# Turning the last x tile of each later chunk on the DMA queue instead of on TensorE, with its values moved one step

## The chip, the cores and the metric

The kernel runs on one core of a Trainium2 chip. The metric is the device time of one execution in microseconds (us). All runs told here are fast runs (granted TensorE clock 0.998 to 1.0). A ratio is the mean time of one kernel's fast runs over that of the other's fast runs of the same rounds, so it isn't quite the ratio of the medians that stand beside it; the 95% interval follows in brackets.

## The reference, cut to what matters

Attention over a band of 64 positions plus 8 global ones, then a gated feed-forward block with a residual:

```python
attn = softmax(where(band | is_global, scale * q @ k.T, -1e9)) @ v
x = attn.transpose(0, 2, 1, 3).reshape(4608, 512)     # B*S tokens, H*D
ffn = (gelu(x @ w_gate) * (x @ w_val)) @ w_out
out = x + sigmoid(x @ w_res) * ffn
```

(Shortened. B, H, S, D = 8, 8, 576, 64; the feed-forward width is 1536.)

## The kernel before: the parts that matter

The 4608 tokens are worked through in nine chunks (c = 0 to 8) of four tiles of 128 tokens. While TensorE does the feed-forward block of chunk c, the attention of chunk c+1 is slipped in between. For each tile t of the next chunk, `values` multiplies the attention weights with v into the PSUM tile `nd`, VectorE divides `nd` and writes `xtok` (tokens on partitions), and `turn_x` makes the transposed `xt`, which the next chunk's `g_ps` and `v_ps` products read.

```python
psn = ctx.enter_context(tc.tile_pool(name="psn", bufs=1, space=PSUM))   # nd: one buffer of two banks
...
def local_values(c, t):
    if split(c, t):          # tiles 0 and 2 of chunk 0: two banks of the matmul ring
        nds = [psm.tile([128, 512], F32, name=f"nd{hf}", tag="mm") for hf in range(2)]
    else:
        nd = psn.tile([128, 2, 512], F32, name="nd", tag="nd")
...
def turn_x(c, t):
    mine = xt[c % 2][:, :, 128 * t:128 * t + 128]
    if c > 1 and t < 3:
        nc.sync.dma_start(mine, xtok[c % 2][:, t, :], transpose=True)
        return
    tx = pss.tile([128, NKT, 128], BF16, name="tx", tag="sc")
    for kk in range(NKT):
        nc.tensor.transpose(tx[:, kk, :], xtok[c % 2][:, t, 128 * kk:128 * kk + 128], ident)
    (nc.vector.tensor_copy if c or t == 3 else nc.scalar.copy)(mine, tx)
...
# the tail of chunk c: 16 steps work_f[n] of four matmuls each,
# gate, third, third, third for each of the four tiles
for n in range(16):
    for w in jobs[n]:
        w()
    work_f[n]()
```

In the traces here TensorE and SyncE start their instructions in the order in which they were emitted (in the first experiment below, a turn whose data are ready stands 2.4 us behind a store). To turn a tile is to transpose it. A gate's four matmuls write the PSUM tile `r_ps`, and a tile's three thirds add up in `f_ps`. The last third of tile t (work_f[4t + 3]) also emits VectorE's `prb`, GpSimd's `ob` and the output store on SyncE's queue, which is the queue of the transposing DMAs too.

The softmax here doesn't subtract the row's maximum and nothing guards it: scores larger than these inputs give would overflow.

## Time and profile before

| | before |
|---|---|
| median, first three runs | 394.37 us (393.6 to 395.18) |
| span of the profiled run | 392.0 us |
| TensorE (PE) busy | 378.8 us, 97% |
| transposes of x on TensorE | 60, of which 28 for tile 3 of chunks 2 to 8 |
| from the first g_ps of chunk 2 to that of chunk 3 | 40.69 us |

The table is read from the top down: TensorE is the bound, so a change pays only by what it does to TensorE's sequence of starts. The last row is the measure that I use throughout: it holds one whole chunk with one tail, and it repeats to some hundredths of a microsecond, while whole runs differ by 1.5 us. The lines themselves stand in the prediction. In them PEld is TensorE loading weights, SPq is SyncE issuing DMAs, and instructions in a row of one kind are merged, with their count (x8). A DMA raises its semaphore sixteen times; its landing is the time of the sixteenth increment.

### The profile page before, as it was taken

What the parts mean: (1) busy time and instruction counts of PE and PEld (TensorE: products, weight loads), DVE (VectorE), ACT (ScalarE), POOL (GpSimd) and SP (SyncE); (2) the same over time, 40 slices, a digit from 0 to 9 for tenths busy, and PEclk for the clock granted to TensorE, in tenths of its full rate; (3) what the DMA queues carried; (4) which work ended last, traced back from release to release, by engine and by line L of the source; (5) the groups of instructions that cost most, each with busy time, mean ns of one, the idle gap of its engine ahead of it and who ended that gap; (6) DMA issues with size and microseconds to landing.
All of it is one profiled execution on the core that took longest, in us unless ns stands there. A gap on an engine that the chain in (4) does not pass through costs nothing.

```text
span 392.0 us, 8491 instructions
## 1 busy us (share of the span) xinstructions
PE 378.8 (97%) x3360; PEld 196.5 (50%) x3360; DVE 203.4 (52%) x446; ACT 171.1 (44%) x285; POOL 169.2 (43%) x203
## 2 busy tenths in 40 slices
PE   3989989999999999999999999999999999999996
PEld 2674555444644454445544554455445544554444
DVE  7767773547543664357444644555445534553422
ACT  6753685236333633354335533462337233633321
POOL 7878764958265424561466137712501210121012
PEclk9999999999999999999999999999999999999999
DMA  8999999699759913997399829992990310041002
GB/s 245 256 378 358 239 321 207 149 196 152 110 97 151 184 42 110 122 204 82 88 149 185 88 82 131 189 113 80 114 150 16 81 55 0 2 93 57 0 28 81
DMA packets 153002, 52.78 MB, mean 135 GB/s; under 512 B 136386, under 2 KB 143426, under 8 KB 152962
## 3 DMA queue, kind: packets, MB, share of 16 engines
q1 hardware_dynamic: 77024, 41.88, 44.4%
q0 software_dynamic: 75392, 9.84, 43.0%
q8 instruction: 26, 0.43, 0.5%
q10 hardware_dynamic: 546, 0.52, 0.4%
q14 instruction: 14, 0.11, 0.1%
HBM read 39.19 MB, written 9.44 MB: 124 GB/s over the span
## 4 chain that ended last, share of the span: by engine, by line
PE 93%; DVE 3%; ACT 2%; issue 1%; POOL 0%; DVEq 0%; POOLq 0%; ACTq 0%
PE g_ps L630 24%; PE v_ps L630 23%; PE f_ps L686 23%; PE r_ps L656 8%; PE nd L575 4%; PE sc L534 3%; PE nd L587 2%; PE ss L481 1%; PE sg L472 1%; PE tx L610 1%; PE tk L451 1%; PE sc L523 1%; PE tq L451 1%; ACT pt L541 1%; PE sn L510 1%
## 5 line engine op out<-in xcount | busy, mean ns | idle before, releaser
L639 DVE SCALAR_TENSOR_TENSOR ht<-gsb,v_ps 128x512 bf16<-128x512 bf16 x108 | 74.2, 688 | 95.3 <-PE v_ps L630 89.2
L636 ACT ACTIVATE gsb<-g_ps 128x512 bf16<-128x512 f32 x108 | 64.4, 597 | 123.1 <-PE g_ps L630 119.7
L692 POOL TENSOR_TENSOR ob<-prb,xtok 128x512 f32<-128x512 f32 x35 | 40.3, 1155 | 172.0 <-DVE prb L690 172.0
L630 PE MATMUL g_ps<-xt,wg_t 128*128 128x512 bf16 (+1 forms) x456 | 111.9, 368 | 0.0
L630 PE MATMUL v_ps<-xt,wv_t 128*128 128x512 bf16 (+1 forms) x456 | 111.9, 368 | 0.0
L686 PE MATMUL f_ps<-wo_t,ht 128*128 128x512 bf16 x420 | 100.1, 379 | 0.0
L630 PEld LDWEIGHTS <-wv_t 128*128 128x128 bf16 x456 | 43.4, 98 | 49.1
L630 PEld LDWEIGHTS <-wg_t 128*128 128x128 bf16 x456 | 43.3, 98 | 48.9 <-issue 0.3
L686 PEld LDWEIGHTS <-ht 128*128 128x128 bf16 x420 | 38.9, 98 | 38.9
L664 ACT ACTIVATE rsb<-r_ps 128x512 bf16<-128x512 f32 x36 | 21.5, 600 | 71.8 <-PE r_ps L656 71.8
L690 DVE SCALAR_TENSOR_TENSOR prb<-rsb,f_ps 128x512 f32<-128x512 bf16 x35 | 24.0, 686 | 27.5 <-PE f_ps L686 26.0
L656 PE MATMUL r_ps<-wr_t,xt 128*128 128x512 bf16 x144 | 36.8, 379 | 1.0 <-ACT rsb L664 1.0
L541 ACT ACTIVATE pt<-sc 128x512 bf16<-128x512 f32 x64 | 33.3, 615 | 4.9 <-PE sc L534 4.8
L91 POOL DMA_DIRECT2D q_st<-in_q_dram x25 | 21.5, 866 | 18.5 <-DMA qt<-q_st 18.4
L557 DVE TENSOR_TENSOR pt<-pt,maskw 128x512 bf16<-128x512 bf16 x56 | 23.2, 424 | 7.7 <-ACT pt L541 5.8
L575 PEld LDWEIGHTS <-pt 128*128 128x128 bf16 x576 | 22.0, 97 | 9.5 <-PE r_ps L656 0.7
L99 POOL DMA_DIRECT2D ve<-in_v_dram x30 | 25.5, 866 | 0.0
L600 DVE TENSOR_TENSOR xtok<-nd,rden 128x512 bf16<-128x512 f32 x34 | 23.5, 691 | 1.3
L91 POOL DMA_DIRECT2D k_st<-in_k_dram x25 | 21.1, 864 | 4.8 <-DMA kt<-k_st 4.1
L575 PE MATMUL nd<-ve,pt 128*128 128x65 bf16 x320 | 22.5, 193 | 0.6 <-DVE xtok L600 0.6
L599 DVE RECIPROCAL rden<-nd 128x8 f32<-128x8 f32 x34 | 7.0, 207 | 29.3 <-PE nd L587 29.2
L656 PEld LDWEIGHTS <-xt 128*128 128x128 bf16 x144 | 13.5, 97 | 16.0 <-issue 0.9
(174 smaller groups left out, 307.9 us busy)
## 6 DMA issues: line engine op xcount, KB each, us to landing
out_dram<-ob SPq DMA_DIRECT2D x35, 256.0 KB
vo<-ve SPq DMA_DIRECT2D x12, 260.0 KB
q_st<-in_q_dram POOLq DMA_DIRECT2D x20, 128.0 KB, 5.8
k_st<-in_k_dram POOLq DMA_DIRECT2D x20, 128.0 KB, 6.5
ve<-in_v_dram POOLq DMA_DIRECT2D x18, 128.0 KB, 7.0
wo_t<-in_k_dram SPq DMA_DIRECT2D x8, 256.0 KB
vraw<-in_q_dram SPq DMA_DIRECT2D x8, 256.0 KB
extra<-in_moe_w_out_dram SPq DMA_DIRECT2D x4, 512.0 KB
```

The lines of the kernel that those rows point to most:

```text
L91: nc.gpsimd.dma_start(dst[0:n, r, :].rearrange("p (h d) -> p h d", d=D), src[b].rearrange("h s d -> s h d")[128 * r:128 * r + n])
L99: nc.gpsimd.dma_start(t[p0:p1, c, :, 0:D], v[b].rearrange("h s d -> s h d")[s0 + p0:s0 + p1])
L541: nc.scalar.activation(sc if stay else mine, sc, ACTF.Exp, bias=0.0, scale=SCALE)
L575: nc.tensor.matmul(nds[h // 4][:, VG * (h % 4):VG * (h % 4) + VG], view(pt, 0, 128, c0, [[1, 128]]), vw, start=(h % 4 == 0 and e == 0), st ...
L600: nc.vector.tensor_tensor(xtok[c % 2][:, t, :].rearrange("p (a h d) -> p a h d", a=2, d=D), num[:, :, :, 0:D], view(rden, 0, 128, 0, [[4, ...
L630: nc.tensor.matmul(held[what][:, c0:c1], w[:, kk, 128 * j:128 * j + 128], x[:, kk, c0:c1], start=(kk == 0), stop=(kk == NKT - 1))
L636: nc.scalar.activation(held["s"], held["g"], ACTF.Gelu, bias=0.0, scale=1.0)
L639: nc.vector.scalar_tensor_tensor(ht[:, j, :], held["s"], 0.5, held["v"], ALU.mult, ALU.mult)
L656: nc.tensor.matmul(r_ps, xt[c % 2][:, kk, 128 * t:128 * t + 128], wr_t[:, kk, :], start=(kk == 0), stop=(kk == NKT - 1))
L686: nc.tensor.matmul(held["f"], ht[:, j, 128 * t:128 * t + 128], wo_t[:, j, :], start=(j == 0), stop=(j == NFF - 1))
L690: nc.vector.scalar_tensor_tensor(prb, held["r"], 1.0, held["f"], ALU.add, ALU.mult)
L692: nc.gpsimd.tensor_tensor(ob, prb, xtok[c % 2][:, t, :], ALU.add)
```

## The change

Its intent is to take the last transposes of the steady chunks off TensorE, and to let the transposing DMA start early enough that it lands before the next chunk reads it. For that, the values of tile 3 come one step earlier and each turn is emitted right behind its values.

```diff
     def turn_x(c, t):
         mine = xt[c % 2][:, :, 128 * t:128 * t + 128]
-        if c > 1 and t < 3:
+        if c > 1:
             nc.sync.dma_start(mine, xtok[c % 2][:, t, :], transpose=True)
             return
@@
             for t in range(4):
-                jobs[5 + 2 * t].append(lambda t=t: values(c + 1, t))
-                jobs[7 + 2 * t].insert(0, lambda t=t: turn_x(c + 1, t))
+                n = (5, 7, 9, 10)[t]
+                jobs[n].append(lambda t=t: values(c + 1, t))
+                jobs[n].append(lambda t=t: turn_x(c + 1, t))
```

## The prediction

> **What bounds the kernel now.** I read the page's engine rows first, then the chain that ended last, then the costliest groups for the lines that the diff touches, and last the timeline of one chunk's tail, which is where all of the change lies.
>
> ```profile
> PE 378.8 (97%) x3360; PEld 196.5 (50%) x3360; DVE 203.4 (52%) x446; ACT 171.1 (44%) x285; POOL 169.2 (43%) x203
> PEclk9999999999999999999999999999999999999999
> PE 93%; DVE 3%; ACT 2%; issue 1%; POOL 0%; DVEq 0%; POOLq 0%; ACTq 0%
> ...
> L610 PE MATMUL tx<-ident,xtok 128*128 128x128 bf16 x60 | 5.9, 219 | 0.0
> ...
> L611 DVE COPY xt<-tx 128x512 bf16<-128x512 bf16 x12 | 5.1, 424 | 7.1 <-PE tx L610 7.1
> ```
>
> TensorE is busy for 97% of the span at the full clock, and 93% of the chain that ended last is TensorE. So an instruction taken off TensorE is worth its slot there, a new hole on TensorE costs its whole length, and half-idle VectorE gives nothing back by itself. The 60 transposes have 219 ns records, but records of pipelined matmuls overlap: what counts is the distance between starts. Here is the tail in which chunk 4 makes x tiles 2 and 3 of chunk 5 (start, length, engine, operation).
>
> ```profile
> 185.49 0.39 PE L587 MATMUL nd<-vgs,gt 128*128 128x260 bf16 x2
> 185.71 1.89 PE L686 MATMUL f_ps<-wo_t,ht 128*128 128x512 bf16 x8
> 185.91 0.21 DVE L599 RECIPROCAL rden<-nd 128x8 f32<-128x8 f32 x1 [0.24 <-PE nd L587]
> 186.16 0.69 DVE L600 TENSOR_TENSOR xtok<-nd,rden 128x512 bf16<-128x512 f32 x1
> 186.94 0.34 SPq L694 DMA_DIRECT2D out_dram<-ob  x1
> 187.38 2.52 SPq L606 DMA_TRANSPOSE xt<-xtok  x2
> 187.92 0.39 PE L587 MATMUL nd<-vgs,gt 128*128 128x260 bf16 x2
> 189.87 0.39 PE L610 MATMUL tx<-ident,xtok 128*128 128x128 bf16 x4
> 190.09 2.75 PE L686 MATMUL f_ps<-wo_t,ht 128*128 128x512 bf16 x12
> 190.29 0.43 DVE L611 COPY xt<-tx 128x512 bf16<-128x512 bf16 x1 [0.30 <-PE tx L610]
> 192.69 1.03 PE L630 MATMUL g_ps<-xt,wg_t 128*128 128x512 bf16 x4
> ```
>
> The reader is to see three things. The four transposes hold TensorE from 189.87 to 190.09. The two tiles of values follow each other with eight f_ps matmuls between them (185.71 to 187.44, where the next tile's first matmul starts). And VectorE empties the first tile's nd only at 186.16 + 0.69 = 186.85; nd has one buffer, so the next tile may not start before that. With eight matmuls between, it never waits.
>
> There is one place in the kernel before where only four matmuls stand between two such tiles, in the first chunk, and it shows what the new order will look like:
>
> ```profile
> 55.91 1.02 PE L656 MATMUL r_ps<-wr_t,xt 128*128 128x512 bf16 x4
> 56.11 0.21 DVE L599 RECIPROCAL rden<-nd 128x8 f32<-128x8 f32 x1 [1.01 <-PE nd L587]
> 56.41 0.69 DVE L600 TENSOR_TENSOR xtok<-nd,rden 128x512 bf16<-128x512 f32 x1
> ...
> 57.17 0.55 PEld L575 LDWEIGHTS <-pt 128*128 128x128 bf16 x16 [0.73 <-PE r_ps L656]
> 57.20 0.19 PE L575 MATMUL nd<-vo,pt 128*128 128x65 bf16 x1 [0.27 <-PE r_ps L656]
> ```
>
> Four such matmuls take 0.86 us (spacing 0.216 us, as 189.01 to 189.87 in the tail above), so TensorE was free for the next tile at 55.91 + 0.86 = 56.77. It started at 57.20, 0.10 us after xtok ended (56.41 + 0.69 = 57.10). The row names r_ps as releaser, but VectorE's read of nd ended last. The hole is 0.43 us.
>
> **What the Trainium skill says.** "TensorE: Matmul & The Clock Gate", Part 4: PE-mode transpose, puts a 128x128 transpose at about 275 ns in a kernel's context and says that its result lands in PSUM, so that a VectorE copy follows. The copy is here (424 ns), and the record's 219 ns is near; but four transposes take only 0.22 us of TensorE, so the page's figure times 28 would overstate the gain almost fivefold. "Perfetto Trace Analysis", DMA Instruction — HWDGE, says that the reported window of such a DMA ends when the sequencer is free, and that the movement of data lies outside of it. The trace agrees: the rows show 1.22 us of issue, while in the trace's records of semaphore increments the transposes' sixteenth increment comes about 2.4 us after the issue starts (issues at 187.38 and 188.70, landings at 189.80 and 191.14). "DMA: Bandwidth & Descriptors", Silent corruption: two transposing streams in flight at once, wants only transposes of different issuers kept apart; all here are issued by SyncE, so no wait is added.
>
> **The change part by part.** It touches x tile 3 of chunks 2 to 8, seven tails.
>
> 1. Removed from TensorE: 7 x 4 = 28 transposes, 189.87 to 190.09 in this tail, 0.223 us with the third digit of the trace. 7 x 0.223 = 1.56 us, all on the path.
> 2. Removed from VectorE: 7 copies of 424 ns, 3.0 us. Each ended long before its reader (190.72 against 192.69), so it is worth nothing.
> 3. Added to the DMA queue: 7 transposes, 21 to 28, of 1.22 us of SyncE issue each.
> 4. Moved: values of tile 3 come one step earlier, so that between the values of tiles 2 and 3 stand four f_ps matmuls instead of eight; the order of TensorE's instructions in the changed kernel confirms it. From the start of those matmuls to the end of xtok the tail takes 186.85 - 185.71 = 1.13 us, and I find 1.13 in all seven tails, also where tile 2 spans two batches. Add the 0.10 us from xtok's end to the first matmul, as measured in the first chunk, and take off the 0.86 us of work: 0.37 us of hole per tail, 7 x 0.37 = 2.6 us, all on the path. The values and f_ps matmuls themselves only change places.
> 5. Moved too: each transpose on the DMA queue is issued right behind its values; tile 1's now goes ahead of an output store that it used to queue behind. Tiles 0 to 2 have slack either way.
>
> Does tile 3 land in time? The next chunk's first matmul reads all four tiles. In the tail above, with the change: values of tile 3 start at 185.71 + 1.13 + 0.10 = 186.94; from their first matmul to the end of xtok the old tail takes 187.44 to 188.59 + 0.69 = 189.28, 1.84 us, so xtok is ready at 188.78. SyncE has issued tile 2 by then (187.38 + 1.22 = 188.60), so tile 3's issue starts near 188.85 and lands near 191.25. The reader comes at 192.69 - 0.22 + 0.37 = 192.84. That leaves 1.6 us. Some issues on this queue took 1.9 to 2.3 us instead of 1.2 (one in each of three tails), which would eat about 1 us of it. So the transfer is hidden.
>
> Sum: -1.56 + 2.6 = +1.0 us. From 394.37 that is 395.4; I say 395.3.
>
> **The rivals.** First, the plain saving: the hole is not there or is filled, and only the 28 transposes count: 394.4 - 1.6 = 392.8. For it: no tail waits today, and the profile shows TensorE idle for almost nothing. Against it: the single buffer of nd and the first chunk's 0.43 us hole, from the same instructions at the same distance. A part of it could come true if nd were released sooner than in the first chunk.
>
> Second, the new transfer becomes the bound: tile 3 lands after the reader is ready. At 1 us late in every tail it would be +7 us on top, about 402, over 2% only from there on. For it: transposes of q and k, which run beside the loads from GpSimd, hold up those loads for several us (loads of q_st waited 18.4 us in total for them), so landing under traffic is far later than 2.4 us. Against it: in the tails that traffic is over; just after the second transpose of the tail above the DMA share falls to 0.11 and then to 0.00 for a whole microsecond, and of the nine landings that I looked at in four tails before the last, eight came 2.4 to 2.5 us after the issue's start and one 3.3. In the last tail there was one disturbed stretch, with a landing 4.8 us after its issue; a late one there would cost some tenths once.
>
> Third, VectorE or SyncE as the new bound: both have less or hardly more to do (52% busy; SyncE idle between 189.9 and 191.26 in this tail, where the new 1.2 us fits). Worth nothing either way.
>
> **Range and chances.** The two terms that count are each known to about 0.05 us per tail, so the mechanism alone gives +0.4 to +1.6 us. The three runs before spread from 393.6 to 395.18, which is as wide as the effect. I take 393.6 to 396.9 for 8 times in 10. Faster by over 2% would need 7.9 us, more than five times all that is removed: 1%. Slower by over 2% needs a late landing of about 1 us in every tail: 3%. Within 2%: 96%.
>
> **What would show it.** The transposes' group should fall from 60 to 32, the copy's from 12 to 5, the DMA transposes of x rise from 21 to 28. In each tail the first values matmul of tile 3 should start about 1.23 us after the f_ps group before it and not 0.86, with a short wait on VectorE's xtok (or put down to f_ps, which ended about then); a distance of 0.86 would prove step 4 wrong and the first rival right. The first g_ps matmul of each chunk should show no wait on a DMA; if it does, the second rival holds. From the first values matmul of tile 2 to the first g_ps of the next chunk should take 0.15 us longer than before; if the total moves by more than 2 us while this distance does not, something outside of the tails moved.

## The result, and the profile after

| | before | after |
|---|---|---|
| median of 6 runs of the same rounds | 394.27 us (393.6 to 395.18) | 394.65 us (393.96 to 395.36) |
| ratio of fast runs | | 1.001 (0.999 to 1.0029) |
| chunk 2, from first g_ps to first g_ps | 40.69 us | 40.81 us |

Nothing that the whole time can resolve. First the page's rows of engines and of the chain that ended last:

```profile
PE 378.2 (96%) x3332; PEld 194.6 (50%) x3332; DVE 198.3 (51%) x439; ACT 171.0 (44%) x285; POOL 167.9 (43%) x203
PE 81%; DMA 9%; DVE 2%; SPq 2%; POOL 2%; ACT 1%; issue 1%; ACTq 0%; DVEq 0%; POOLq 0%
```

28 matmuls and 7 copies are gone. That the chain has 81% of TensorE now and not 93% is no news of the tails: in order of time, its DMA pieces lie at 1.9 to 51 us, where weights and the first inputs are loaded, and the long pieces after 57.7 us are TensorE's but for two of ScalarE's (3.4 us together, at 337.4 us). The followed chain merely took another branch in the beginning. The groups of the transposes and of their copies:

```profile
L610 PE MATMUL tx<-ident,xtok 128*128 128x128 bf16 x32 | 3.2, 219 | 0.0
...
L611 DVE COPY xt<-tx 128x512 bf16<-128x512 bf16 x5 | 2.1, 423 | 5.0 <-PE tx L610 5.0
```

60 became 32 and 12 became 5, as forecast. The same tail of chunk 4 as in the prediction, in the changed kernel:

```profile
185.60 1.02 PE L686 MATMUL f_ps<-wo_t,ht 128*128 128x512 bf16 x4
...
186.04 0.69 DVE L600 TENSOR_TENSOR xtok<-nd,rden 128x512 bf16<-128x512 f32 x1
186.78 0.54 PEld L575 LDWEIGHTS <-pt 128*128 128x128 bf16 x16 [0.66 <-DVE xtok L600]
186.79 0.20 PE L575 MATMUL nd<-ve,pt 128*128 128x65 bf16 x1 [0.17 <-DVE xtok L600]
186.82 0.34 SPq L694 DMA_DIRECT2D out_dram<-ob  x1
187.27 2.64 SPq L606 DMA_TRANSPOSE xt<-xtok  x2
...
187.51 1.89 PE L686 MATMUL f_ps<-wo_t,ht 128*128 128x512 bf16 x8
...
190.09 2.75 PE L686 MATMUL f_ps<-wo_t,ht 128*128 128x512 bf16 x12
...
192.69 0.81 PE L630 MATMUL g_ps<-xt,wg_t 128*128 128x512 bf16 x3
```

The four f_ps matmuls start at 185.60 and need 0.86 us; tile 3's values start at 186.79, 1.19 us later, right behind the end of xtok (186.04 + 0.69 = 186.73). That is the forecast hole: 1.19 - 0.86 = 0.33 us. The f_ps group of twelve follows the gate directly (no row of tx ahead of it), and g_ps shows no wait. The waits of TensorE, before and then after (total us, times, longest):

```profile
PE nd L575 <- DVE xtok L600: 0.6, 1, 0.6
```

```profile
PE nd L575 <- DVE xtok L600: 1.7, 8, 0.6
```

Seven more waits, one per tail. The view adds only 1.1 us for them, where seven holes of 0.33 are 2.3 us: the f_ps record before each wait has a modelled end that reaches beyond its slot of 0.216 us between starts (0.38 us long), so the view sees only 0.17 us of each hole idle. The distance of starts is the safer reading, and it is the same in all seven tails: 1.19 us, with 0.06 us from the end of xtok to the first values matmul.

### The profile page after: what moved, and what is told of

Its sections match the earlier page's. It is cut to its first block, busy times and chain, and to the rows that moved or that the text cites. A ratio compares the mean times of both kernels' runs of the same rounds, so it can differ in the third digit from the quotient of the medians.

```text
span 392.4 us, 8445 instructions
## 1 busy us (share of the span) xinstructions
PE 378.2 (96%) x3332; PEld 194.6 (50%) x3332; DVE 198.3 (51%) x439; ACT 171.0 (44%) x285; POOL 167.9 (43%) x203
## 4 chain that ended last, share of the span: by engine, by line
PE 81%; DMA 9%; DVE 2%; SPq 2%; POOL 2%; ACT 1%; issue 1%; ACTq 0%; DVEq 0%; POOLq 0%
PE f_ps L686 21%; PE v_ps L630 21%; PE g_ps L630 21%; PE r_ps L656 7%; PE nd L575 4%; DMA extra<-in_moe_w_val_dram 3%; SPq L185 2%; PE nd L587 2%; PE sc L534 2%; DMA wo_t<-in_k_dram 2%; DMA vraw<-in_v_dram 2%; DMA xtok<-in_v_dram 2%; DMA ht<-in_q_dram 1%; DVE xtok L600 1%; PE ss L481 1%
## 5 line engine op out<-in xcount | busy, mean ns | idle before, releaser
L575 PE MATMUL nd<-vo,pt 128*128 128x65 bf16 x256 | 19.9, 193 | 0.9 <-DVE xtok L600 0.5
```

The lines of the kernel that those rows point to most:

```text
L575: nc.tensor.matmul(nds[h // 4][:, VG * (h % 4):VG * (h % 4) + VG], view(pt, 0, 128, c0, [[1, 128]]), vw, start=(h % 4 == 0 and e == 0), st ...
```

## The experiments

All ran five rounds against the kernel before; each gave the right result. The diffs are against the changed kernel if nothing else is said. For the comparison here is chunk 2 of every run, and what its difference from before makes times seven tails, beside the measured medians.

| run | chunk 2, us | (difference) x 7 | median, before beside it | ratio (95%) |
|---|---|---|---|---|
| before | 40.69 | | | |
| after | 40.81 | +0.8 | 394.65, 394.27 | 1.001 (0.999 to 1.0029) |
| e1_old_places | 42.25 | +10.9 | 405.7, 394.25 | 1.0291 (1.0272 to 1.0311) |
| e2_values_at_11 | 40.47 | -1.6 | 392.61, 394.25 | 0.996 (0.994 to 0.9979) |
| e3_values_move_alone | 41.04 | +2.4 | 396.84, 394.25 | 1.0063 (1.0043 to 1.0082) |
| e4_other_banks | 40.49 | -1.4 | 392.68, 394.25 | 0.9965 (0.9948 to 0.9983) |
| e5_values_at_12 | 41.56 | +6.0 | 400.13, 394.08 | 1.0145 (1.0128 to 1.0162) |
| e6_stores_elsewhere | 40.47 | -1.6 | 392.45, 394.08 | 0.9957 (0.9942 to 0.9971) |

The theory at the start: per tail, the transposes give back 0.22 us, the hole takes 0.33 us, and the transfer is hidden. The rivals: no hole (something else took the gain), or a transfer that lands late.

### The DMA turn at the old places

```diff
-                n = (5, 7, 9, 10)[t]
-                jobs[n].append(lambda t=t: values(c + 1, t))
-                jobs[n].append(lambda t=t: turn_x(c + 1, t))
+                jobs[5 + 2 * t].append(lambda t=t: values(c + 1, t))
+                jobs[7 + 2 * t].insert(0, lambda t=t: turn_x(c + 1, t))
```

> All four x tiles of chunks 2 to 8 on the DMA queue, but values and turns emitted at the old places (values of tile 3 one step later again, each turn two steps behind its values). My theory: there is no hole between the values of tiles 2 and 3 (distance from the f_ps group to the values of tile 3 back to 1.72 us), but the turn of tile 3 now stands behind tile 2's output store on SyncE's queue, is issued about 191.7 on the time scale of chunk 4's tail, lands 2.4 us later at 194.1, and its reader is ready at 192.5: TensorE waits about 1.7 us for a DMA in each of seven tails. 7 x (1.7 - 0.22) = +10 us on the kernel before, about 404.5 us (400 to 408). Rival, the DMA's landing is hidden wherever its turn is emitted and only the 28 transposes count: 392.8 us.

Measured: 405.7 us. The tail of chunk 4 in this run, SyncE's queue and the reader:

```profile
195.21 0.34 SPq L694 DMA_DIRECT2D out_dram<-ob  x1
195.66 1.21 SPq L606 DMA_TRANSPOSE xt<-xtok  x1
...
198.36 0.81 PE L630 MATMUL g_ps<-xt,wg_t 128*128 128x512 bf16 x3 [1.78 <-DMA xt<-xtok]
```

The turn goes out behind the store, 2.4 us after its xtok was ready (192.54 + 0.69 = 193.23 in the same timeline), and TensorE waits 1.78 us for it; the waits view has 11.8 us in seven such waits. So a late landing costs TensorE in full, and with the turns where they were the change would have been 2.9% slower.

### The values of tile 3 at step 11

```diff
-                n = (5, 7, 9, 10)[t]
+                n = (5, 7, 9, 11)[t]
```

> As the changed kernel, but values and turn of tile 3 one step later (11 in place of 10), so eight f_ps matmuls stand between the values of tiles 2 and 3 as in the kernel before. My theory (the hole of 0.33 us per tail is what took the gain, and the transfer has slack): no hole, the turn is issued at about 189.35, lands at 191.75 before its reader at 192.47; the whole 7 x 0.223 = 1.56 us comes out: 392.7 us, ratio to the kernel before 0.996. Rival A (the gain was lost to something else, such as DMA traffic, queue order or VectorE): 394.5 us as the changed kernel. Rival B (0.7 us of slack isn't enough): g_ps waits for a DMA, above 395 us.

Measured: 392.61 us, ratio 0.996. The tail:

```profile
185.99 1.89 PE L686 MATMUL f_ps<-wo_t,ht 128*128 128x512 bf16 x7
...
187.71 0.19 PE L575 MATMUL nd<-ve,pt 128*128 128x65 bf16 x1
...
187.92 2.91 SPq L606 DMA_TRANSPOSE xt<-xtok  x2
...
192.74 1.03 PE L630 MATMUL g_ps<-xt,wg_t 128*128 128x512 bf16 x4
```

Eight f_ps matmuls (one record is missing from the trace) take 187.71 - 185.99 = 1.72 us with no hole, and g_ps waits for nothing. The second of the two transposes, tile 3's, is issued at 189.64 and its sixteenth semaphore increment is recorded at 192.05, 0.7 us before g_ps. That slack is not large: tile 3 landed 2.4 to 2.9 us after its issue in all ten runs that turn it on the queue, but single transposes of tiles 0 to 2 in the changed kernel took 4.0 to 4.2 us, and a tile 3 as late as that would be past it. On TensorE this run and the one before it have the same order; they differ only in where the turns stand in SyncE's queue, and that is worth 13 us. One digit makes the change the gain that it was meant to be, and this version beats the kernel before by 0.4% (interval 0.2 to 0.6), and the changed one as well (394.65 us, in other rounds).

### The move of the values alone

```diff
-        if c > 1:
+        if c > 1 and t < 3:
             nc.sync.dma_start(mine, xtok[c % 2][:, t, :], transpose=True)
@@
-                jobs[n].append(lambda t=t: turn_x(c + 1, t))
+                jobs[n if t < 3 else 13].append(lambda t=t: turn_x(c + 1, t))
```

> The values of tile 3 stand at the new place (10) but tile 3 is turned on TensorE at the old place (13), as in the kernel before. My theory: the hole alone, 7 x 0.33 = +2.3 us on the kernel before, 396.6 us, ratio 1.006. Rival (the new place costs nothing, what took the gain is the added DMA): 394.3 us, ratio 1.000.

Measured: 396.84 us, ratio 1.0063, 2.6 us over before.

```profile
187.39 1.02 PE L686 MATMUL f_ps<-wo_t,ht 128*128 128x512 bf16 x3
...
187.83 0.69 DVE L600 TENSOR_TENSOR xtok<-nd,rden 128x512 bf16<-128x512 f32 x1
188.58 0.20 PE L575 MATMUL nd<-ve,pt 128*128 128x65 bf16 x1 [0.16 <-DVE xtok L600]
```

The same distance of 1.19 us, without the added DMA. So the hole belongs to the move of the values, and by itself it costs more than the transposes give back. This and the run at step 11 are the two parts of the change by themselves: +2.6 and -1.6 us, +1.0 together, and the change measured +0.4 with an interval of about -0.4 to +1.1.

### The same order, another buffer

```diff
     def split(c, t):
-        return c == 0 and t % 2 == 0
+        return c == 0 and t % 2 == 0 or c > 1 and t == 2
@@
-                nc.vector.tensor_tensor(xtok[0][:, t, 256 * hf:256 * hf + 256]...
+                nc.vector.tensor_tensor(xtok[c % 2][:, t, 256 * hf:256 * hf + 256]...
```

> As the changed kernel, order and places kept, but the values of tile 2 of chunks 2 to 8 go into two banks of the matmul ring instead of the single nd buffer (VectorE then empties them in two halves, about 0.35 us more of VectorE). My theory (the hole is the wait for VectorE's read of the single nd buffer): the hole between tiles 2 and 3 goes, distance from the f_ps group to the values of tile 3 0.86 us; the gain of 1.56 us comes out, 392.7 us, ratio 0.996; perhaps some hundredths per tail lost to a wait for a ring bank. Rival (the hole has another cause, such as loading weights behind the wait for the masked scores): the distance stays 1.19 us and the time 394.6 us.

Measured: 392.68 us, ratio 0.9965.

```profile
185.30 1.02 PE L686 MATMUL f_ps<-wo_t,ht 128*128 128x512 bf16 x3
...
186.16 0.19 PE L575 MATMUL nd<-ve,pt 128*128 128x65 bf16 x1
```

The distance is 0.86 us though the values stand at step 10 as in the change: with tile 2 in other banks, tile 3 need not wait for VectorE (which was busy with tile 2 until 186.56 here). The order was never the trouble by itself; the single buffer was. Whether one moves the instruction or the buffer gives the same 1.6 us.

### The values of tile 3 at step 12

```diff
-                n = (5, 7, 9, 10)[t]
+                n = (5, 7, 9, 12)[t]
```

> Values and turn of tile 3 one step later than in the best place so far (12 in place of 11). On the time scale of chunk 4's tail of the run with 11: xtok of tile 3 ends at 190.4, and the turn now stands behind tile 2's output store, which waits for GpSimd until about 190.7. My theory (a store ahead in the queue holds the turn up, and landing comes 2.4 us after the issue's start): issue 191.14, landing 193.55, reader ready at 192.74: TensorE waits some 0.85 us in each of seven tails, 392.7 + 6 = 398.7 us. Rival (the store ahead does not matter, only when xtok is ready): issue 190.5, landing 192.9, 392.7 + 1.5 = 394.2 us.

Measured: 400.13 us, 1.4 us over what I had expected, with the rival 6 us away.

```profile
192.99 0.34 SPq L694 DMA_DIRECT2D out_dram<-ob  x1
193.44 1.21 SPq L606 DMA_TRANSPOSE xt<-xtok  x1
...
196.01 0.81 PE L630 MATMUL g_ps<-xt,wg_t 128*128 128x512 bf16 x3 [0.94 <-issue]
```

From tile 3's first values matmul (190.74) the turn was issued after 2.70 us, not 2.57, as the store ahead of it came later than I had reckoned; it landed 2.48 us after the issue (195.92), not 2.41; and the reader would have been ready at about 194.9, so TensorE lost 1.1 us, not 0.85. The mechanism held and each of its lengths was a little short. The row says "issue" where a DMA ended the wait, and so do three of the seven tails in the waits view (the other four name the DMA): with a wait this close behind a landing the profile's guess at the releaser isn't firm.

### The stores on another queue

Against the first experiment (old places):

```diff
-                    nc.sync.dma_start(out[r0:r0 + 128, :], ob)
+                    (nc.gpsimd if c else nc.sync).dma_start(out[r0:r0 + 128, :], ob)
```

> The run with the old places (405.7 us), but the output stores of chunks 1 to 8 are issued by GpSimd right behind its own addition, so that no store stands ahead of a turn in SyncE's queue; order on TensorE unchanged. My theory (the 1.7 us per tail are the queue order, not the transfer itself): the turn of tile 3 is issued as soon as xtok is ready and the time falls to about that of the run with 11, 392.7 us, at most 393.5 if GpSimd's later loads cost something. Rival (the lateness belongs to the transfer or to the place of emission, whatever is ahead of it): it stays near 405 us.

Measured: 392.45 us against 405.7 with the stores on SyncE's queue.

```profile
183.57 6.09 SPq L606 DMA_TRANSPOSE xt<-xtok  x3
...
187.72 0.69 DVE L600 TENSOR_TENSOR xtok<-nd,rden 128x512 bf16<-128x512 f32 x1
...
191.59 0.59 PE L630 MATMUL g_ps<-xt,wg_t 128*128 128x512 bf16 x2
```

The turns are emitted at the same late places, but nothing waiting stands ahead of them: in chunk 4's tail xtok of tile 3 ends at 187.72 + 0.69 = 188.41, the turn (the last of the three) is issued at 188.47 and landed at 190.88, before the reader at 191.59. The lateness was the queue's order, not the transfer.

### The first tail too

The first chunk's tail has the hole that the prediction was taken from. Against the run with step 11, one f_ps group goes ahead of the values of tile 1 and one ahead of those of tile 3:

```diff
-            values(1, 1)
             third(0, 0)
+            values(1, 1)
@@
-            values(1, 3)
             third(1, 1)
+            values(1, 3)
```

> The run with 11, and in the first chunk's tail one f_ps group moved ahead of the values of tile 1 and one ahead of those of tile 3, so that eight matmuls stand between two tiles of values there too. My theory of the hole (one nd buffer, about 1.13 us from the group's start to xtok's end, plus 0.06): the two holes there (0.43 and about 0.26 us) go and 0.7 us comes off: 392.0 us, ratio to the kernel before 0.994. Rival (other waits of the first tail take their place): 392.7 us, as the run with 11.

Measured: 392.1 us, ratio 0.9944 (0.9926 to 0.9963), not told apart from the run with step 11 by these runs. In the trace the first tail, from the first values matmul of tile 0 to the first g_ps, went from 15.84 to 15.17 us: both holes closed. But chunk 1 then took 41.10 us in place of 40.36. The start of chunk 1 in this run:

```profile
69.36 0.61 POOL L205 CAST q_st<-vraw 128x512 bf16<-128x512 f32 x1 [5.15 <-PE f_ps L686]
69.94 4.49 POOL L692 TENSOR_TENSOR ob<-prb,xtok 128x512 f32<-128x512 f32 x4
...
71.12 0.69 DVE L690 SCALAR_TENSOR_TENSOR prb<-rsb,f_ps 128x512 f32<-128x512 bf16 x1 [1.88 <-POOL ob L692]
...
71.87 1.02 PE L630 MATMUL g_ps<-xt,wg_t 128*128 128x512 bf16 x4
```

GpSimd stood before a cast that needs a load of q (the row names f_ps, but the load's last increment comes at 69.21 us, 0.15 us before the cast, the same distance as in the other profiles); the four additions queued behind it, VectorE's prb waited for them (two buffers), and the PSUM banks came free late: g_ps at 71.87 should have started at 71.74. About half of the 0.74 us was lost by the v_ps group that follows, the rest at the turn of the global keys later in the chunk. So a version was tried with that cast behind the additions, beside repeats of the other two:

```diff
-            cast_second("q", 0, 1, POOL)
@@
-            cast_second("q", 1, NQT, POOL)
+            cast_second("q", 0, NQT, POOL)
```

> As the run with both holes of the first tail closed, but GpSimd's first cast of q for chunk 2 stands behind its four additions of the first tail, not ahead of them. My theory: in that run the cast waited for q's load until 69.4, the four additions queued behind it, VectorE's prb waited for them with two buffers, and TensorE waited 0.74 us in chunk 1 for the banks, which gave back the 0.67 us of the two holes. With the cast behind, chunk 1 takes 40.4 us again in place of 41.1 and the whole is 0.7 us under the run with 11: 391.9 us against 392.6, both beside the same runs of before. Rival (the time given back in chunk 1 has another cause): chunk 1 stays at 41.1 us and the time is that of the run with 11.

> The run with 11 again, so that it stands beside the next two on one chip: ratio 0.996 once more, chunk 1 40.4 us.

> The run with the first tail's holes closed, again: my theory says that its loss in chunk 1 comes back in a second profile (0.3 to 0.8 us, as q's load ends on its own clock), so that it is at most 0.3 us under the run with 11. If the loss was chance in one profile, it is 0.7 us under.

| run | first tail, us | chunk 1, us | cast ahead of chunk 1's first g_ps, us | median, before 394.39 | ratio (95%) |
|---|---|---|---|---|---|
| e8_cast_later | 15.17 | 40.37 | (behind it) | 391.65 | 0.9937 (0.9924 to 0.9951) |
| e9_eleven_again | 15.84 | 40.76 | 1.06 | 392.37 | 0.9955 (0.9941 to 0.9968) |
| e10_first_tail_again | 15.17 | 40.37 | 2.58 | 392.1 | 0.9939 (0.9925 to 0.9954) |
| the first run with both holes closed | 15.17 | 41.10 | 0.65 | 392.1, other rounds | 0.9944 (0.9926 to 0.9963) |

My expectation that the loss in chunk 1 would come back in the repeat was wrong: it did not. It came in the repeat of the run with step 11 instead, at 0.40 us. What the runs show is a race between q's load, which ends at its own time, and TensorE: the cast started 0.65 us ahead of chunk 1 where 0.74 us were lost, 1.06 us ahead where 0.40 were lost, 1.42 us ahead where 0.20 were lost (the move of the values alone), and 1.68 us (the kernel before) or more ahead where nothing was.

The banks are only half of the cause. In the repeat of the run with step 11 all of the 0.40 us goes at TensorE's turn of the global queries (`tg`), which starts 17.71 us after chunk 1's first g_ps in place of 17.32. It waits for rows that GpSimd gathers behind the same additions and casts: that gather was issued at 12.19 us and landed at 17.40, against 11.05 and 16.36 in the repeat with both holes closed. With the cast behind the additions the loss was not there in the one profile of it, but the gather landed at 16.94. By the 0.31 us from landing to `tg` just seen it may come at 17.01 at the latest, so less than 0.1 us was to spare: that the loss can't come back is not shown. (That profile lost 0.25 us in chunk 3, 40.62 in place of 40.36 us, where TensorE waited for a transpose of k.) That version has the lowest median, 391.65 us, but its interval overlaps with the others'.

## Why the prediction was right

- **The bound** (TensorE at 97%, so only its sequence counts): right. VectorE lost 7 copies (5.1 to 2.1 us in their group; 203.4 to 198.3 in all), and it bought nothing: the move of the values alone, which keeps the copies, is slower than the change by 0.23 us in chunk 2, and that is the transposes' 0.223.
- **Step 1, 0.223 us per tail for the transposes**: right. The run with step 11 shortens chunk 2 by 0.22 us.
- **Step 4, the hole**: right in kind and place; its size was 0.33 and not 0.37 us. The term that was off is the 0.10 us from the end of xtok to the first values matmul: in the tails it is 0.06 us (186.73 to 186.79). I had measured it at the one place where the kernel before showed it, and there the first matmul has other waits as well (for GpSimd's part of v and for a DMA); that these made up the rest was not tested. With 0.33 us the prediction's own sum is 7 x (0.33 - 0.223) = +0.75 us.
- **Step 3 and the landing**: right. Counted from the start of the f_ps group before tile 3's values (185.71 in the profile before, 185.60 in the one after), the issue was forecast at 3.14 us and came at 3.12, the landing at 5.54 and came at 5.53, the reader at 7.13 and came at 7.09, without a wait. The slack was 1.56 us against a forecast 1.6, in one of the seven tails 1.13. The sample behind it was too kind: of all eighteen landings in the six tails before the last, three (all tile 0's) came 3.3 to 3.5 us after the issue, where the prediction has one of nine. Step 5, the queue order, which I had weighed only for tiles 0 to 2, turned out to be what the slack hangs on: at the old places the same turn costs 2.9%.
- **The sum**: +1.0 us forecast; +0.4 measured in the times (interval about -0.4 to +1.1), in the trace +0.11 to +0.12 us for each of six chunks and +0.06 for the seventh, +0.7 together. (In the seventh it was the kernel before that was 0.05 us slower than in its other tails.) The hit by itself says little: the stated range also holds a change that is worth nothing. What bears the mechanism out are the distances and the runs with and without the hole.
- **The rivals**: the plain saving (392.8) is what the three runs without hole and late landing show, 392.5 to 392.7, so it was the right number for another kernel. The late landing did not occur here, and does where a store stands ahead.

## What to carry to other kernels

When work is taken off the bound engine, look at what its neighbours are now next to: an instruction that moves closer to the last user of a single buffer turns that buffer into a wait, and here it ate more than was saved; one more group of matmuls between, or another bank, was the whole difference between +0.4 and -1.6 us. A DMA is late not by its own length alone but by what stands ahead of it in its issuer's queue, so emit it ahead of stores that still wait for another engine. And measure such changes by the distance between two starts on the bound engine within one steady period: it resolves 0.1 us where whole runs scatter by 1.5.

## What the Trainium skill lacked or had wrong

- "TensorE: Matmul & The Clock Gate", Part 4: PE-mode transpose, gives a duration only (about 275 ns in a kernel). What a transpose takes from a busy TensorE is its slot: four 128x128 transposes took 0.223 us, 0.056 us each, with records of 219 ns.
- The same page, Back-to-back issue gap, gives about 131 ns per matmul at N=512 and 81 ns at N=128 for sustained streams in a real kernel, and says that its isolated formula (N/2.4 + 2.5, in ns) counts too much at 512 and too little at 128. In this kernel's stream groups of four N=512 matmuls start 0.86 us apart, 216 ns for each, in every trace here, and the transposes 56 ns each: the isolated formula fits both.
- "DMA: Bandwidth & Descriptors", Latency and other measured facts, has no time from issue to landing for a transposing DMA within SBUF, and I found none elsewhere for this size. For 128x512 elements of 2 bytes the issue mostly took 1.2 us. In the changed kernel 21 of 28 such transposes landed 2.39 to 2.46 us after the issue's start and the other seven 2.7 to 4.2 us; in the kernel before the slowest took 4.8 us.
- On no page did I find the time from the end of a VectorE write to the start of a matmul that waits for it: 0.06 us in the seven tails here, 0.10 us at a place with further waits.
